# First batch's attention with keys on partitions, its maxima entered as a row and its probabilities kept in float32

## The chip, the core and the metric

The kernel runs on one core of a Trainium2 chip. The metric is the device time of one execution in microseconds (us). The engines of the core are named as the profile names them: PE (TensorE, matrix products; PEld is its weight loads), DVE (VectorE), ACT (ScalarE), POOL (GpSimd) and SP, whose queue issues the DMA transfers here. Each engine works through its own instructions in the order in which the built program lists them and waits on semaphores for the others.

## What is computed

```python
def _attn_ref(q, k, v, g_q, g_k):            # q, k, v: (4, 12, 448, 64)
    def rmsnorm(x, g):
        rms = np.sqrt(np.mean(x * x, axis=-1, keepdims=True) + 1e-06)
        return x / rms * g
    q_n, k_n = (rmsnorm(q, g_q), rmsnorm(k, g_k))
    scores = (1.0 / np.sqrt(64)) * np.matmul(q_n, k_n.transpose(0, 1, 3, 2))
    scores = scores - np.max(scores, axis=-1, keepdims=True)
    attn = np.exp(scores)
    attn = attn / (np.sum(attn, axis=-1, keepdims=True) + 1e-09)
    return np.matmul(attn, v).astype(np.float32)
...
x = attention, reshaped to (1792, 768)
g = x @ w_gate; x = (g * (1 / (1 + np.exp(-g))) * (x @ w_val)) @ w_out      # d_ff 1536
h = x @ w_in;   x = (h * np.cos(h)) @ w_out                                 # d_ff 2048
```

The weights arrive as 64-bit floats, and the kernel rebuilds 32-bit floats from their bits. Products are made to float32 accuracy from pairs of 16-bit parts ("hi" and "lo").

## The kernel before, in words

Batch 0's attention is computed first. Then, for each batch b, the first expansion layer of batch b (pieces of gate, val and out1 weights, `mm_piece`, lines 826 to 834) is recorded together with the attention of batch b+1. At the end come the second layer's `h` products and its output. A batch has six pairs of heads (g = 0 to 5 for batch 0, 6 to 11 for batch 1), a pair has seven tiles of 128 query rows (64 of each head of the pair), and n counts the tiles.

The recording loop calls `step(n, b)`, in which tables of offsets (`OFF`, chosen by `PH`) place the preparation of each pair, and `DEL` the steps behind the scores. After the recording a scheduler of the framework sets the final order on each engine by its own model of durations and by when buffers of the pools come free. So a changed table or pool moves instructions on all engines. `CF` holds a string of flags for each batch, which say what engine does an optional step.

For one pair of batch 0 the steps before are these:

- Preparation: `p_load`, `p_vload`, squares and row sums (`p_sq`), a power on POOL (`p_pow`, 305), scaling (`p_mul`, 342/343/345; times the gains, 352), splits in hi and lo (357 to 377), a DMA transpose of q and k (`p_T`), and `p_sw`, which copies the transposed q with its halves exchanged to W (388, 389). `p_vhi` and `p_vlo` split v (396, 405).
- Scores, queries on partitions: four products of 64 columns each (`s_mm`, 419), the maximum of each row over the keys on DVE (`s_max`, 428), which is turned into a bias (430), and the exponential with the bias and with a running sum (`s_exp`, 438).
- Probabilities: split in hi and lo (`s_phi`, 462 on ACT or 464 on DVE; `s_plo`, 471 on POOL or DVE), transposed by DMA so that keys lie on partitions (`s_pt`), and multiplied with the split v (`a_av`, 530).
- The reciprocals of the sums are spread over the partitions by a float32 product with ones (`a_sum` and `a_r`, 491, 503, 505), and `a_x` scales the result (540) and splits it (545 to 549) into the tile xy, X[g], which the first layer reads.

PSUM has eight banks: four of the pool ps_m (`mm`, the first layer), one of ps_t (`t`, the attention's output) and three of ps_s (`s`, scores and small products). All pools live for the whole program, so a piece of batch 0's first layer may run as soon as the three X tiles it reads are there.

Of the kernel before, what the change touches and what calls it, by code (L numbers as in the profile page):

```python
# [27 lines left out]
VM1 = 2  # L28
VMQ = 2
# [35 lines left out]
 {'load': -7,  # L65
  'vload': -6,
  'sqk': -5,
  'sqq': -5,
  'pow': -4,
  'mul': -3,  # L70
  'khi': -2,
  'klo': -2,
  'qhi': -2,
  'qlo': -2,
  'T': -1,
  'vhi': -1,
  'vlo': -1,
  'sw': -1},
# [42 lines left out]
PH = (1, 1, 1, 1, 0, 1, 3, 4, 5)  # L121
# [12 lines left out]
def kernel(ctx: ExitStack, tc, q, k, v, g_q, g_k, w_gate, w_val, w_out, w2_in, w2_out, out):  # L134
# [31 lines left out]
    ps_m = ctx.enter_context(tc.tile_pool(name="ps_m", bufs=4, space=PSUM))  # L166
# [31 lines left out]
    vsc = const.tile([P, 2 * B], F32, name="vsc")  # L198
    ynrm = const.tile([P, B * KX], F32, name="ynrm")
# [5 lines left out]
    junk = const.tile([P, S], BF16, name="junk")  # L205
# [61 lines left out]
    def p_load(g):  # L267
        rqk = pool("raw", g).tile([P, 2, NS, D], F32, tag="rqk", name="rqk")
        nc.sync.dma_start(rqk[:, 1], rows7(k, g))
        nc.sync.dma_start(rqk[:, 0], rows7(q, g))  # L270
        prep[g] = dict(rqk=rqk)

    def p_vload(g):
        rv = pool("rv", g).tile([P, 2, NS, D], F32, tag="rv", name="rv")
        b, p = divmod(g, NP)
        vs = v[b, 2 * p:2 * p + 2].rearrange("h (q t) d -> q h (t d)", t=NS)
        rv2 = rv.rearrange("p h t d -> p h (t d)")
        nc.sync.dma_start(rv2[:HP], vs)
        nc.sync.dma_start(rv2[HP:, :, :S - D], vs[:, :, D:])
        if "vw" in cfg(g):  # L280
# [27 lines left out]
    def v_max(b):  # L308
# [19 lines left out]
        nc.vector.tensor_copy(vsc[:, 2 * b:2 * b + 2], ps[:, :2])  # L328

# [54 lines left out]
    def p_sw(g):  # L384
# [3 lines left out]
        nc.vector.tensor_copy(W[:HP], T[HP:, :NS])  # L388
        nc.vector.tensor_copy(W[HP:], T[:HP, :NS])
# [160 lines left out]

    PREP = (
# [10 lines left out]
    LEAD = -min(OFF[ph(g)][nm] + NS * g for g in range(NP) for nm, f in PREP)  # L562

    def s_prep(n):
        for nm, f in PREP:
            for g in range(NPAIR):
                if NS * g + OFF[ph(g)][nm] == n:
                    f(g)
# [13 lines left out]
    def step(n, b):  # L582
        if NB * b <= n < NB * (b + 1):
# [298 lines left out]
    def fin_out1(b, c, ps):  # L882
        for f in range(2):
# [3 lines left out]
            nc.scalar.activation(junk[:, :S], t, AF.Square, accum_out=ynrm[:, b * KX + kt:b * KX + kt + 1])  # L887
# [112 lines left out]
    open_pool(start_ctx, **A0)  # L1000
    gtmp = start_ctx.enter_context(tc.tile_pool(name="gtmp", bufs=1)).tile([P, D], F32, name="gtmp")
    emit_consts(gtmp)
    step(-LEAD, 0)
# [11 lines left out]
    start_ctx.close()  # L1015
    g_ctx = ctx.enter_context(ExitStack())
# [154 lines left out]
```

## Time and profile before

| | |
|---|---|
| time of three runs, median (lowest to highest) | 1394.31 us (1391.92 to 1395.64) |
| the profiled execution | 1392.76 us |
| its span, first to last instruction | 1391.0 us |
| busy: PE, DVE, ACT, POOL | 1181.6, 879.5, 654.6, 440.6 us |

The profile is one execution on the chip. A row of a group names the line, the engine, the operation, what it writes and reads, the shapes, how many there are, the time that they kept the engine busy, and the mean of one. The granted clock of PE is given as a share of 2.4 GHz. Busy time over the whole span says little, because the program has stages with different limits: batch 0's attention alone, batch 0's first layer beside batch 1's attention, the same for the later batches, and the second layer.

### The profile page before, as it was taken

Reading aid. Unit: us, or ns where it says so; the run is one execution under the profiler, and the core shown is the slowest. Engines: PE = TensorE matmul, PEld = TensorE weight load, DVE = VectorE, ACT = ScalarE, POOL = GpSimd, SP = SyncE. Lnnn points to the kernel's source line nnn. Section 1 sums busy time; section 2 is a strip of 40 time slices with the busy share of each in tenths; the row PEclk is TensorE's granted clock in tenths of the full one; section 3 lists DMA queues with packets and bytes.
Section 4 is the critical chain, followed back from the end, with each engine's and each line's share of the span. In section 5 each row is a group of like instructions: output and inputs, shape, how many; then the busy total and the mean of one; then the engine's idle time right before and its main releaser. Section 6 shows DMA issues by size and latency. Waiting matters only on the chain. (4 is left out here: it accounts for less than half of the span.)

```text
span 1391.0 us, 18432 instructions
## 1 busy us (share of the span) xinstructions
PE 1181.6 (85%) x6448; PEld 671.3 (48%) x6448; DVE 879.5 (63%) x1633; ACT 654.6 (47%) x1324; POOL 440.6 (32%) x340
## 2 busy tenths in 40 slices
PE   1267587776789799998989999995999999999998
PEld 0122233333565344773436855772455555666665
DVE  7988879989995777547755178547777775200000
ACT  3677454656342456535554336446677776200000
POOL 4767635534851245314332011101323233000000
PEclk9877778788999899999999999997999999999999
DMA  9699677877899899999999998863100012633221
GB/s 260 174 202 209 158 222 206 215 202 200 238 341 354 169 237 222 246 355 223 207 231 226 305 324 285 292 215 102 35 12 12 24 57 63 221 120 101 63 87 40
DMA packets 297149, 259.28 MB, mean 186 GB/s; under 512 B 210016, under 2 KB 241760, under 8 KB 297056
## 3 DMA queue, kind: packets, MB, share of 16 engines
q1 hardware_dynamic: 297056, 258.11, 66.6%
q8 instruction: 50, 0.82, 0.3%
q14 instruction: 43, 0.35, 0.1%
HBM read 163.64 MB, written 44.87 MB: 150 GB/s over the span
## 5 line engine op out<-in xcount | busy, mean ns | idle before, releaser
L832 PE MATMUL mm<-xy,wp 128*128 128x448 f16 x960 | 347.7, 364 | 22.6 <-DVE tmp L868 7.5
L833 PE MATMUL mm<-xy,wp 128*128 128x448 f16 x960 | 348.1, 363 | 0.0
L834 PE MATMUL mm<-xy,wp 128*128 128x448 f16 x960 | 341.4, 362 | 4.4 <-DVE wp L702 4.4
L471 POOL TENSOR_TENSOR p<-pr,p 128x448 f16<-128x448 f32 x114 | 141.2, 1245 | 180.7 <-ACT p L462 94.8
L845 PEld LDWEIGHTS <-g 128*128 128x128 f16 x1344 | 131.5, 98 | 87.3
L438 ACT ACTIVATE pr<-s,sm,esc 128x448 f32<-128x448 f32 x168 | 120.0, 716 | 81.5 <-DVE sm L432 58.4
L832 PEld LDWEIGHTS <-wp 128*128 128x128 f16 x960 | 97.3, 102 | 117.8 <-issue 28.3
L833 PEld LDWEIGHTS <-wp 128*128 128x128 f16 x960 | 96.4, 100 | 102.6 <-issue 26.1
L834 PEld LDWEIGHTS <-wp 128*128 128x128 f16 x960 | 94.7, 100 | 101.8 <-issue 10.9
L977 POOL TENSOR_TENSOR g<-tmp,g 128x448 f16<-128x448 f32 x64 | 68.8, 1094 | 226.7 <-ACT g L976 144.6
L419 PE MATMUL s<-T 128*64 128x448 f16 x336 | 71.7, 416 | 52.3 <-ACT pr L438 37.6
L832 PE MATMUL mm<-g,wp 128*128 128x448 f32 x288 | 108.7, 377 | 6.4 <-ACT wp L772 5.4
L834 PE MATMUL mm<-g,wp 128*128 128x448 f32 x288 | 105.6, 375 | 7.7 <-POOL wp L773 7.7
L833 PE MATMUL mm<-g,wp 128*128 128x448 f32 x288 | 106.7, 370 | 0.0
L879 POOL TENSOR_TENSOR g<-tmp,g 128x448 fp32r<-128x448 f32 x48 | 60.8, 1275 | 144.4 <-ACT g L878 144.1
L428 DVE TENSOR_REDUCE sm<-s 128x1 f32<-128x448 f32 x168 | 100.3, 613 | 5.9 <-PE s L419 5.5
L845 PE MATMUL s<-wp,g 128*128 128x384 f16 x576 | 100.3, 326 | 0.0
L845 PE MATMUL mm<-wp,g 128*128 128x384 f16 x576 | 99.1, 326 | 0.0
L305 POOL TENSOR_TENSOR ri<-ss,half 128x14 f32<-128x14 f32 x24 | 65.2, 2719 | 74.0 <-DVE ss L303 51.3
L462 ACT ACTIVATE p<-pr 128x448 f16<-128x448 f32 x132 | 73.1, 569 | 22.5 <-DMA PT<-p 19.3
L669 DVE TENSOR_SCALAR w<-raw 128x768 int32<-128x768 int32 x68 | 45.1, 667 | 53.3 <-DMA raw<-in_moe_w_out_dram 49.6
L670 DVE SCALAR_TENSOR_TENSOR w<-raw,w 128x768 int32<-128x768 int32 x68 | 75.1, 1112 | 0.7
(136 smaller groups left out, 1868.9 us busy)
## 6 DMA issues: line engine op xcount, KB each, us to landing
wp<-scr_out SPq DMA_DIRECT2D x96, 384.0 KB, 4.5
raw<-in_moe_w_out_dram SPq DMA_DIRECT2D x28, 768.0 KB, 6.5
wp<-scr_gate SPq DMA_DIRECT2D x36, 384.0 KB, 5.2
wp<-scr_val SPq DMA_DIRECT2D x36, 384.0 KB, 5.3
raw<-in_moe_w_in_dram SPq DMA_DIRECT2D x16, 768.0 KB, 6.2
raw<-in_moe_w_gate_dram SPq DMA_DIRECT2D x12, 768.0 KB, 5.3
raw<-in_moe_w_val_dram SPq DMA_DIRECT2D x12, 768.0 KB, 5.5
scr_out<-wp SPq DMA_DIRECT2D x24, 384.0 KB, 5.9
```

Source lines behind the costliest of these rows:

```text
L305: nc.gpsimd.tensor_tensor(ri.rearrange("p a b -> p (a b)"), ss, half[:, :2 * NS], op=ALU.pow)
L419: nc.tensor.matmul(ps[hs, :S].rearrange("p (t q) -> p t q", q=HP), (T, W)[i][:, t, hs], T[:, NS:, hs], start=(i == 0), stop=(i == 1),)
L428: nc.vector.tensor_reduce(sm[:, 0, t:t + 1], slot[n][:, :S], axis=AX.X, op=ALU.max)
L438: nc.scalar.activation(e, slot.pop(n)[:, :S], AF.Exp, bias=sm[:, 1, t:t + 1], scale=esc, accum_out=sm[:, 2, t:t + 1],)
L462: nc.scalar.activation(hi, slot[n], AF.Copy)
L471: eng.tensor_sub(p16[:, t - t0, 1], slot.pop(n), p16[:, t - t0, 0])
L670: nc.vector.scalar_tensor_tensor(wi, hi, -0x40000000, wi, op0=ALU.bitwise_and, op1=ALU.bitwise_or)
L832: nc.tensor.matmul(ps[f][:, :S], wh[:, s], x[:, 0], start=(first and i == 0), stop=False)
L833: nc.tensor.matmul(ps[f][:, :S], wh[:, s], x[:, 1], start=False, stop=False)
L834: nc.tensor.matmul(ps[f][:, :S], wl[:, s], x[:, 0], start=False, stop=(last and i == n - 1))
L845: nc.tensor.matmul(ps[:, :CO], x[:, a, p0:p0 + P], rhs, start=st, stop=sp)
L977: nc.gpsimd.tensor_sub(x[:, 1], r, x[:, 0])
```

## The change

Batch 0's attention gets a path of its own (`c_step` and the functions `c_*`); batches 1 to 3 keep theirs.

- `c_s` makes a tile of scores with queries on partitions as before, with two products in place of four, for the maximum alone. `c_row` takes the seven maxima of a pair, splits them in two 16-bit parts, turns them into rows with seven small products against an identity, and ACT copies them under the transposed q (B, rows 64 to 127).
- `c_st` makes the scores again, now with keys on partitions: one product for the hi parts and one for the lo part of k and the maxima's rows in the same 128 rows of contraction. ACT takes the exponential and writes it in float32. No split, no DMA transpose of the probabilities and no running sum.
- `c_av` multiplies the float32 probabilities with v and with ones, both as float32 products. The sums so arrive already spread over the partitions, in a bank of their own (u). `c_x` adds 1e-9, takes the reciprocal of the whole 128x448 tile on DVE, and scales.
- For batch 0 the gains and the lo part of k go to POOL, v is not split, and k is loaded head by head.
- `CF` of batch 1 changes too: the copies of W go to ACT (`sa`), all tiles' hi parts of the probabilities to ACT, R's copy (505) and the hi part of x (545) to ACT, the last part of v to a DMA, and the lo part of x (549) to POOL; the lo parts of k and q and one lo tile of the probabilities come to DVE; and q's scaling (343) moves to POOL.
- The four ps_m banks are opened only after batch 0's attention; until then three banks ps_c and one ps_u take their place.
- `fin_out1` squares in place in PSUM, and the tile `junk` is gone.

```diff
-A0 = {'raw0': 2, 'rv0': 1, 'h160': 1, 'T0': 1, 'p160': 3, 'pr0': 4, 'sq0': 3}
+A0 = {'raw0': 2, 'rv0': 2, 'h160': 1, 'sq0': 1, 'pr0': 6, 'T0': 1}
+COL = {'B': 3, 'C': 3, 'w': 3, 'r': 1}
...
-CF = ('rp rv vw ql vh nm xl qm qd qe b c e 2', 'rp rv vw ql vh nm xh kl qd qe c d e', 'ql xl 0 2 5 6', 'ql xl 0 3 4 6')
+CF = ('kl xl ql qm kg', 'rp vh nm xl qm sa 2', 'ql xl 0 2 5 6', 'ql xl 0 3 4 6')
...
+CAV = 1
+CXX = 8
+CSM = 10
+CRW = 2
+CSH = 10
...
-PH = (1, 1, 1, 1, 0, 1, 3, 4, 5)
+PH = (2, 2, 2, 2, 2, 2, 3, 4, 5)
...
-    ps_m = ctx.enter_context(tc.tile_pool(name="ps_m", bufs=4, space=PSUM))
...
-        nc.vector.tensor_copy(W[:HP], T[HP:, :NS])
-        nc.vector.tensor_copy(W[HP:], T[:HP, :NS])
+        if "sa" in cfg(g):
+            nc.scalar.activation(W[:HP], T[HP:, :NS], AF.Copy)
+            nc.scalar.activation(W[HP:], T[:HP, :NS], AF.Copy)
+        else:
+            nc.vector.tensor_copy(W[:HP], T[HP:, :NS])
+            nc.vector.tensor_copy(W[HP:], T[:HP, :NS])
...
+    def c_copy(g):
...
+        nc.vector.tensor_copy(Bq[:HP], T[HP:, :NS])
+        nc.vector.tensor_copy(T[HP:, :NS], T[:HP, :NS])
+        nc.scalar.activation(C[:HP], T[:HP, NS:], AF.Copy)
+
+    def c_s(n):
...
+        for h in range(2):
+            hs = slice(HP * h, HP * h + HP)
+            nc.tensor.matmul(ps[hs, :S].rearrange("p (t q) -> p t q", q=HP), T[:, t, hs], T[:, NS:, h::2], start=True, stop=True)
+        nc.vector.tensor_reduce(pg["m"][:, 0, t:t + 1], ps[:, :S], axis=AX.X, op=ALU.max)
+
+    def c_row(g):
...
+        nc.vector.tensor_scalar(W[:, :, 0], m, 2.0 ** -14, None, op0=ALU.mult)
+        nc.vector.scalar_tensor_tensor(W[:, :, 32], m, 2.0 ** -14, W[:, :, 0], op0=ALU.mult, op1=ALU.subtract)
+        for t0, t1 in ((0, 4), (4, NS)):
+            ps = bank(ps_s, "s")
+            for t in range(t0, t1):
+                nc.tensor.matmul(ps[HP:, (t - t0) * P:(t - t0 + 1) * P], W[:, t], id16, start=True, stop=True)
+            nc.scalar.activation(
+                pg["B"][HP:, t0:t1], ps[HP:, :(t1 - t0) * P].rearrange("p (t q) -> p t q", q=P), AF.Copy,
+            )
+
+    def c_st(n):
...
+        for k, (wt, off, mv) in enumerate(((T, NS, T), (C, 0, Bq))):
...
+                nc.tensor.matmul(
+                    ps[rows, :S].rearrange("p (t q) -> p t q", q=HP), w, mv[:, :NS, hs], start=(k == 0), stop=(k == 1),
+                )
+        nc.scalar.activation(e, ps[:, :S], AF.Exp, scale=esc)
+
+    def c_av(g, j):
...
+        for dst, v_of in ((pg["o"], True), (pg["u"], False)):
+            for h in range(2):
...
+                nc.tensor.matmul(dst[hs, :S], w, e[rows], start=(j == 0), stop=(j == 3))
+
+    def c_x(g):
...
+        nc.vector.tensor_scalar(r, pg["u"][:, :S], 1e-9, None, op0=ALU.add)
+        nc.vector.reciprocal(r, r)
...
+        nc.vector.scalar_tensor_tensor(xs, pg["o"][:, :S], vs2, r, op0=ALU.mult, op1=ALU.mult)
+        nc.scalar.activation(x[:, 0], xs, AF.Copy)
+        nc.gpsimd.tensor_sub(x[:, 1], xs, x[:, 0])
...
-            nc.scalar.activation(junk[:, :S], t, AF.Square, accum_out=ynrm[:, b * KX + kt:b * KX + kt + 1])
+            nc.scalar.activation(ps[f][:, :S], ps[f][:, :S], AF.Square, accum_out=ynrm[:, b * KX + kt:b * KX + kt + 1])
...
     start_ctx.close()
+    ps_m = ctx.enter_context(tc.tile_pool(name="ps_m", bufs=4, space=PSUM))
```

What the built programs list shows the moves at three places. The first is PE in the middle of batch 0's attention, where probabilities meet v. Before (t is the output, PT the transposed probabilities, vh the hi part of v):

```order
L419 MATMUL s<-T,W 64x448
L419 LDWEIGHTS W
L419 MATMUL s<-T,W 64x448
L530 LDWEIGHTS vh
L530 MATMUL t<-PT,vh 64x448
```

After (pr are the float32 probabilities, rv is v, c the transposed scores):

```order
L641 LDWEIGHTS T
L641 MATMUL c<-T 128x448
L641 LDWEIGHTS cC
L641 MATMUL c<-cB,cC 128x448
L658 MATMUL t<-pr,rv 64x448
L658 MATMUL u<-pr,full 64x448
```

Where a run of 16-bit products stood (22 of line 530 for a pair), whose two halves of columns alternate, two float32 products for the same half of the columns (line 658, one to t and one to u) now follow each other, and 128-column score products stand between them and the next two.

The second place is DVE where a pair of batch 0 ends. Before (R spreads the reciprocals, p are the split probabilities):

```order
L487 TENSOR_SCALAR sm<-sm 128x7
L505 COPY R<-s 128x448
L488 RECIPROCAL sm<-sm 128x7
L428 TENSOR_REDUCE sm<-s 128x1 x2
L464 CAST p_754<-pr 128x448
L464 CAST p_787<-pr 128x448
L471 TENSOR_TENSOR p_787<-pr,p_787 128x448
L540 SCALAR_TENSOR_TENSOR tmp<-t,R 128x448
```

After (cr is the new tile of reciprocals, sm the maxima):

```order
L663 TENSOR_SCALAR cr<-u 128x448
L309 TENSOR_REDUCE ss<-sq 128x7
L612 TENSOR_REDUCE sm<-s 128x1
L664 RECIPROCAL cr<-cr 128x448
L612 TENSOR_REDUCE sm<-s 128x1
L598 COPY cB<-T 64x896
L309 TENSOR_REDUCE ss<-sq 128x7
L612 TENSOR_REDUCE sm<-s 128x1 x2
L667 SCALAR_TENSOR_TENSOR tmp<-t,vs_102,cr 128x448
```

The casts and the subtraction are gone, the reciprocal is over 448 elements in place of 7, and maxima of later tiles queue behind it.

The third place is PE where the first layer begins. Before, in the middle of batch 0's attention (mm are the first layer's banks, wp its weights):

```order
L503 MATMUL s<-R,ones 128x448
L832 LDWEIGHTS wp
L832 MATMUL mm<-xy,wp 128x448
L833 LDWEIGHTS wp
L833 MATMUL mm<-xy,wp 128x448
```

After, at the end of batch 0's attention:

```order
L658 MATMUL t<-pr,rv 64x448 x2
L658 MATMUL u<-pr,full 64x448 x2
L843 MATMUL s<-nm,full 128x1
L979 LDWEIGHTS wp
L979 MATMUL mm<-xy,wp 128x448
L980 LDWEIGHTS wp
L980 MATMUL mm<-xy,wp 128x448
```

All of the first layer's products now stand behind the last of batch 0's attention, where in the program before they were interleaved with its second half.

## Rows read from the trace of the kernel before

**Rows 1.** Stages: window, length, busy time of each engine (instructions), PEclk, DMA share, GB/s.

```profile
0.00:157.00 157.00, 70.71 (x372) 28.86 (x373) 133.43 (x242) 92.78 (x220) 102.36 (x86) 0.83 0.88 207
157.00:425.00 268.00, 198.83 (x970) 108.36 (x968) 242.34 (x375) 136.15 (x298) 141.69 (x92) 0.84 0.83 230
425.00:900.00 475.00, 441.80 (x2463) 261.72 (x2464) 301.38 (x656) 224.40 (x477) 127.77 (x98) 0.97 0.93 260
```

**Rows 2.** Timeline of DVE: batch 0's first and last scaling by the reciprocals.

```profile
84.37 0.62 DVE L540 SCALAR_TENSOR_TENSOR tmp<-t,R 128x448 f32<-128x448 f32 x1
...
156.74 0.62 DVE L540 SCALAR_TENSOR_TENSOR tmp<-t,R 128x448 f32<-128x448 f32 x1
```

**Rows 3.** Groups by line, DVE, 0 to 425 us: busy, mean ns | idle before.

```profile
L428 DVE TENSOR_REDUCE sm<-s 128x1 f32<-128x448 f32 x89 | 53.2, 612 | 3.3 <-PE s L419 2.9
...
L464 DVE CAST p<-pr 128x448 f16<-128x448 f32 x36 | 22.1, 616 | 3.5 <-ACT pr L438 3.2
...
L405 DVE SCALAR_TENSOR_TENSOR vl<-rv,vsc,vh 128x256 f16<-128x256 f32 x28 | 19.3, 722 | 2.8 <-ACT sq L295 1.6 <-ACT vh L396 1.2
L345 DVE TENSOR_TENSOR rqk<-rqk,ri 128x896 f32<-128x896 f32 x10 | 15.5, 1547 | 0.6 <-POOL ri L305 0.6
L352 DVE TENSOR_TENSOR rqk<-rqk,gk 128x448 f32<-128x448 f32 x16 | 14.9, 929 | 0.1
L389 DVE COPY W<-T 64x896 f16<-64x896 f16 x14 | 10.7, 762 | 0.2
L388 DVE COPY W<-T 64x896 f16<-64x896 f16 x14 | 9.6, 683 | 3.0 <-DMA T<-h 2.6
...
L505 DVE COPY R<-s 128x448 f32<-128x448 f32 x12 | 7.4, 615 | 3.6 <-PE s L503 3.5
...
L363 DVE TENSOR_TENSOR h<-rqk,h 128x448 f16<-128x448 f32 x9 | 7.1, 793 | 0.0
L471 DVE TENSOR_TENSOR p<-pr,p 128x448 f16<-128x448 f32 x8 | 6.9, 864 | 1.3 <-ACT p L462 1.2
L487 DVE TENSOR_SCALAR sm<-sm 128x7 f32<-128x7 f32 x12 | 5.8, 481 | 0.1
L342 DVE TENSOR_TENSOR rqk<-rqk,ri 128x448 f32<-128x448 f32 x6 | 5.5, 924 | 0.0
L281 DVE COPY rv<-rv 64x128 f32<-64x128 f32 x12 | 5.0, 416 | 2.0 <-DMA rv<-in_v_dram 1.7
L549 DVE TENSOR_TENSOR xy<-tmp,xy 128x448 f16<-128x448 f32 x6 | 4.4, 736 | 0.0
...
L545 DVE CAST xy<-tmp 128x448 f16<-128x448 f32 x6 | 2.9, 489 | 0.0
L488 DVE RECIPROCAL sm<-sm 128x7 f32<-128x7 f32 x12 | 2.3, 190 | 0.1
L681 DVE RECIPROCAL wsc<-winv 128x1 f32<-128x1 f32 x12 | 1.9, 157 | 0.2
```

**Rows 4.** Timeline of PE: a float32 product at either clock, and pairs behind one.

```profile
73.53 1.83 PE L503 MATMUL s<-R,ones 128*128 128x448 f32 x2 [0.22 <-ACT pr L438]
75.30 0.58 PE L419 MATMUL s<-T 128*64 128x448 f16 x2
75.67 0.42 PE L419 MATMUL s<-T,W 128*64 128x448 f16 x2
...
200.88 0.92 PE L503 MATMUL s<-R,ones 128*128 128x448 f32 x2
201.63 0.28 PE L696 MATMUL s<-nm,full 128*128 128x1 f32 x2
```

**Rows 5.** Groups by line, ACT, 0 to 425 us: a copy of 896 columns.

```profile
L396 ACT ACTIVATE vh<-rv,vsc 128x896 f16<-128x896 f32 x12 | 12.3, 1034 | 2.6 <-PE t L530 2.0 <-DVE rv L281 0.6
```

**Rows 6.** Timeline of DVE: one copy of W while POOL is idle.

```profile
37.81 0.39 DVE L388 COPY W<-T 64x896 f16<-64x896 f16 x1
```

**Rows 7.** DMA issues, 0 to 157 us: count and median us to landing.

```profile
PT<-p SPq DMA_TRANSPOSE x24, 4.3
```

More of the change, by code (lines that the diff above doesn't have):

```diff
@@ L64 @@
   'sw': -5},
[L65 to L78, printed above, removed]
+ {'load': -23,
+  'vload': 2,
+  'sqk': -18,
+  'sqq': -18,
+  'pow': -15,
+  'mul': -15,
+  'khi': -15,
+  'klo': -11,
+  'qhi': -14,
+  'qlo': -9,
+  'T': -3,
+  'vhi': -10,
+  'vlo': -4,
+  'sw': -2},
  {'load': -13,
@@ L198 @@
     vsc = const.tile([P, 2 * B], F32, name="vsc")
+    vs2 = const.tile([P, 1], F32, name="vs2")
+    id16 = const.tile([P, P], F16, name="id16")
     ynrm = const.tile([P, B * KX], F32, name="ynrm")
@@ L549, in a_x, with ctile, c_const @@
         eng.tensor_sub(x[:, 1], xs, x[:, 0])
+    col = {}
+    colc = {}
+    CT = [(0, 0), (1, 0), (0, 1), (1, 1), (0, 2), (1, 2), (None, 3)]
+    def ctile(nm, shape, dt, g=None):
+        return c_p.tile(shape, dt, tag="c" + nm, name="c" + nm, bufs=COL[nm])
+    def c_const(i):
+        C = ctile("C", [P, NS, P], F16)
+        nc.vector.memset(C[HP:], 0.0)
+        for r in (HP, HP + 32):
+            nc.vector.memset(C[r:r + 1], -(2.0 ** 14))
+        W = ctile("w", [P, NS, HP], F16)
+        nc.vector.memset(W, 0.0)
+        colc[i] = (C, W)
@@ new lines, in c_st @@
+    def c_st(n):
+        g, i = divmod(n, NS)
+        pg = prep[g]
+        T, Bq, C = pg["T"], pg["B"], colc[g % 3][0]
+        ps = bank(ps_c, "c")
+        h0, j = CT[i]
+        e = col[g, i] = pool("pr", g, n).tile([P, S], F32, tag="pr", name="pr")
+        for k, (wt, off, mv) in enumerate(((T, NS, T), (C, 0, Bq))):
+            for h in ((0, 1) if h0 is None else (h0,)):
+                hs = slice(HP * h, HP * h + HP)
+                rows = hs if h0 is None else slice(0, P)
+                k0 = (off + 2 * j) * P + h
+                w = wt.rearrange("p t q -> p (t q)")[:, k0:min(k0 + 2 * P - 1, (off + NS) * P):2]
+                nc.tensor.matmul(
+                    ps[rows, :S].rearrange("p (t q) -> p t q", q=HP), w, mv[:, :NS, hs], start=(k == 0), stop=(k == 1),
+                )
+        nc.scalar.activation(e, ps[:, :S], AF.Exp, scale=esc)
@@ new lines, in c_av @@
+    def c_av(g, j):
+        pg = prep[g]
+        if j == 0:
+            pg["o"] = bank(ps_t, "t")
+            pg["u"] = bank(ps_u, "u")
+        rv = pg["rv"]
+        for dst, v_of in ((pg["o"], True), (pg["u"], False)):
+            for h in range(2):
+                hs = slice(HP * h, HP * h + HP)
+                rows = slice(0, P) if j < 3 else hs
+                e = col[g, 2 * j + h] if j < 3 else col[g, NS - 1]
+                w = rv[rows, h, 2 * j if j < 3 else NS - 1 - h] if v_of else full[rows, :HP]
+                nc.tensor.matmul(dst[hs, :S], w, e[rows], start=(j == 0), stop=(j == 3))
@@ L560, in ph @@
         return PH[g if g < NP else NP - 1 + g // NP]
-    LEAD = -min(OFF[ph(g)][nm] + NS * g for g in range(NP) for nm, f in PREP)
+    LEAD = -min(OFF[ph(g)][nm] + NS * g - CSH for g in range(NP) for nm, f in PREP)
     def s_prep(n):
@@ L582, in step @@
     def step(n, b):
-        if NB * b <= n < NB * (b + 1):
+        if b == 0:
+            c_step(n)
+        elif NB * b <= n < NB * (b + 1):
             s_mm(n)
@@ L1000 @@
     open_pool(start_ctx, **A0)
+    ps_c = start_ctx.enter_context(tc.tile_pool(name="ps_c", bufs=3, space=PSUM))
+    ps_u = start_ctx.enter_context(tc.tile_pool(name="ps_u", bufs=1, space=PSUM))
+    c_p = start_ctx.enter_context(tc.tile_pool(name="cp", bufs=1))
     gtmp = start_ctx.enter_context(tc.tile_pool(name="gtmp", bufs=1)).tile([P, D], F32, name="gtmp")
     emit_consts(gtmp)
+    for i in range(3):
+        c_const(i)
     step(-LEAD, 0)
```

62 lines of the change are left out of this document (57 added, 5 removed).

## The prediction

> **What bounds the kernel now.** First the table of stages [rows 1]. Until 157 us batch 0's attention runs nearly alone, until 425 us batch 0's first layer runs beside batch 1's attention, and from then on PE is busy 442 of 475 us at a clock of 0.97. In the first two stages DVE is the fullest engine: 133 of 157 us (85%) and 242 of 268 us (90%); PE has 71 and 199 us, ACT 93 and 136, POOL 102 and 142. A later stage that is full of PE work starts when the earlier ones end, so what is saved before 425 us should come out at the end nearly one to one. Then the pace within the first stage: batch 0's first pair is scaled at 84.4 us and its sixth at 156.7 [rows 2], so a pair takes 14.5 us. Then the groups of DVE [rows 3]: their idle time in front is small nearly everywhere, so DVE sets the pace by the work in its list. The question is therefore how much DVE work the change takes out before 425 us, and whether PE, which gets slow float32 products, takes over as the bound.
>
> **DVE, batch 0.** Removed for six pairs, each count times its mean [rows 3]: 18 casts of probabilities x 0.616 = 11.1 us, 6 subtractions (471) x 0.864 = 5.2, 12 lo parts of v (405) x 0.722 = 8.7, 6 products with the gains (352) x 0.929 = 5.6 and 6 lo parts of k (363) x 0.793 = 4.8, which both go to POOL, 6 copies of R (505) x 0.615 = 3.7, 6 additions to the sums (487) x 0.481 = 2.9, 6 small reciprocals x 0.190 = 1.1, 6 copies of v's last part (281) x 0.416 = 2.5. Together 45.6 us. The seven maxima of a pair (428), the scaling and two copies of 64x896 stay in kind and number. Added: 6 additions of 1e-9 over 128x448, like line 505, 3.7 us; 12 operations on 128x7 at about 0.2, 2.4 us; and 6 reciprocals over 128x448, which no row shows. Their bounds: 0.615 us, if a reciprocal runs like the copy of that size, and, by the slope between the reciprocal of one element (0.157) and of seven (0.190), 0.0055 us for an element, 0.15 + 448 x 0.0055 = 2.6 us. I take 2.6, because it rests on the same operation: 15.7 us. The memsets of the new constants stand at the very start, where DVE waits for the first loads; I take nothing, and up to 3 us if they are not covered. Net: 45.6 - 21.8 = 23.8 us less.
>
> The Trainium skill (VectorE: DVE Perf Modes, First, the fixed hardware budget) speaks against this part: it says that a reciprocal runs an iterated divide with a repeat count of 8, and gives DVE's clock as 0.96 GHz. By that an estimate is 448 x 8 / 0.96 GHz = 3.7 us for one and 6.6 us more for the six; no row here shows that size.
>
> **DVE, batch 1.** Removed: 18 casts, 11.1 us; 6 times the two copies to W (0.683 + 0.762), 8.7, which ACT takes over; 6 copies of R, 3.7; v's last part, 2.5; x's hi part (545) 6 x 0.489 = 2.9 and lo part (549) 6 x 0.736 = 4.4; the smaller scaling (1.547 - 0.924) x 6 = 3.7. Together 37.0 us. Added: lo parts of k and q, 12 x 0.793 = 9.5, and 6 subtractions x 0.864 = 5.2. Net 22.3 us less. Both batches: **46 us** of DVE work less, all before 425 us. The ends, with the reciprocal at 0.6 us and with uncovered memsets (3 us) beside a sum that is 10% off: 58 and 38.
>
> **Where it is missing.** Counting both lists of DVE to batch 0's last scaling, with these means, the new one is only about 8 us shorter there, because the conversion of weights and batch 1's preparation have moved ahead of it; by the end of the first layer's conversions the whole difference is there. So 8 us belong to the first stage and some 38 to the second.
>
> **PE, stage one.** A float32 product of 448 columns takes [rows 4] 1.77 us at the half clock (73.53 to 75.30) and 0.75 us at the full one (200.88 to 201.63). A 16-bit pair in the two column halves takes 0.37 us at the half clock (75.30 to 75.67) and half of that, 0.19, at the full one. A pair of heads had 14 + 11 such pairs and one float32 product: 25 x 0.19 + 0.75 = 5.5 us at the full clock. It now has 7 pairs of products for the maxima, 14 for the transposed scores, seven small ones (about 0.1 us each) and 16 float32 products, in the order that follows each tile's exponential, t and u for the same half of the columns in a row, so I count them one after the other: 21 x 0.19 + 0.7 + 16 x 0.75 = 16.7 us at the full clock and 21 x 0.37 + 0.7 + 16 x 1.77 = 37 us at the half clock. If t and u for different halves did overlap, as the 16-bit pairs do, it would be 10.7 and 23. For six pairs 100 us at the full clock, 221 at the half. The room for it is about 120 us: from the first scores, which come later (I take 30 us, since POOL does two more steps of the first pairs' preparation), to some 150. At the full clock that is 83% of the room; at the half clock it is far too much. The row of the stage [rows 1] has a clock of 0.83, that is about a third of the time at 1.2 GHz, for a PE that was busy 71 of 157 us. With PE busy most of the time I expect more of the full clock, and that PE and DVE become about equally tight. So I give the first stage nothing: the last scaling at about 157 us as before, where DVE alone would give 157 - 8 = 149.
>
> **Other engines and queues.** PE's first layer for batch 0 can no longer begin inside the first stage, since its banks are opened behind it; what moves is 72 products x 0.19 = 14 us of PE work into a stage with 199 of 268 us busy. ACT loses the running sums, biases and splits of batch 0 and gains in batch 1: 18 hi parts (0.57), 12 copies of W at most 1.03 each (the nearest row, line 396 [rows 5], has all partitions), 6 copies of R and 6 of x; some 28 us on 136. POOL loses batch 0's subtractions and gains three smaller steps. SP loses batch 0's 24 transposes of probabilities [rows 7], which delayed nobody but their own pair. The squares in PSUM (887) hold a bank some half microsecond longer, beside PE work on the other banks: nothing.
>
> **Sum.** Second stage: PE would have 199 + 14 us in 268 - 38 = 230 us (93% at the old clock, less if the clock rises), ACT 164 of 230. With three engines that full in fixed orders not all of DVE's 38 us will come through; I take four fifths, 30 us, because DVE's 90% is still above PE's share at a better clock. The profiled execution took 1392.76 us: 1392.8 - 0 - 30 = **1363 us**. The median of the runs shown is 1.5 us above that execution, well within what I can claim; 0.3% (4 us) is about what a measurement of this kernel can tell from no change.
>
> **Rivals.**
>
> More comes through: PE keeps the full clock in stage one and the last scaling comes at about 149, and the second stage yields its whole 38 us: 46 us, 1347 us. DVE's own operations may get shorter too: a copy to W takes 0.39 us while POOL is idle [rows 6] against a mean of 0.683 [rows 3], and POOL loses work; some 6 us, 1341. For it: DVE's small idle times. Against it: PE's 83%.
>
> Less comes through: in the second stage the first layer's pieces wait for weights, ACT and PE in turn, the DMA share is 0.83 already and the same bytes have to come in less time. Then about 10 us remain: 1383 us.
>
> Slower: PE becomes the bound of stage one at the half clock. Each float32 product waits for its tile's exponential and is followed by a wait for the next, so that PE is never busy for long. With a share s of the work at the half clock it has 100 + 121 s us; started at 30 us and with 7 us behind it, the last scaling comes at 137 + 121 s. It is at 157 for s = 0.17, and the second stage's 30 us are used up at 187, s = 0.41. With s = 0.55 it is 204, 47 - 30 = 17 us slower: 1410 us. For it: a third of this stage ran at the half clock. Against it: PE had less than half the work.
>
> No change: what the first stages gain is lost again after 425 us, for instance to a DMA share of 0.93 [rows 1]: 1392 us. Against it: PE is 93% busy there.
>
> **How the numbers follow.** Forecast, 1352 to 1376: 0.47. More: 0.17. Less: 0.16. No change: 0.06. Slower: 0.14. The likeliest case gives 1363. Leaving out the slower case and a tail of the greater gain, the range is 1340 to 1393, in which the unknown reciprocal (up to 12 us less) lies too. Faster 0.47 + 0.17 + 0.16 = 0.80, the same 0.06, slower 0.14.
>
> **What would show it.** Right: the reciprocal of 128x448 at about 2.6 us; float32 products for t and u some 0.75 us apart at the full clock; a clock above 0.83 until the last scaling, which comes between 145 and 168 us; the first piece of batch 1's first layer some 30 us earlier; the stage after that unchanged in length. Wrong: the last scaling beyond 187 us with a clock near 0.7 (slower), DVE well under 85% in the second stage with waits for PE or DMA in its place (less), or a stage after 425 us that grows by what was gained.

## The result, and the profile after

The changed kernel takes 1374.97 us (median of four runs, 1374.25 to 1379.06) against 1394.17 us (median of four): a ratio of 0.987, 95% interval 0.9846 to 0.9893, so 19 us faster. The forecast was 1363 us (1352 to 1376 for its likeliest case), the range 1340 to 1393. The profiled execution took 1375.23 us, its span is 1373.1 us.

The stages of the changed kernel, in the windows of [rows 1] and with the same columns:

```profile
0.00:157.00 157.00, 98.47 (x422) 32.68 (x423) 112.74 (x203) 73.10 (x127) 68.71 (x55) 0.97 0.51 143
157.00:425.00 268.00, 227.68 (x1166) 125.04 (x1163) 233.24 (x346) 160.84 (x346) 135.17 (x90) 0.90 0.89 251
425.00:900.00 475.00, 434.55 (x2406) 262.35 (x2405) 308.80 (x665) 223.69 (x475) 129.95 (x97) 0.96 0.93 263
```

In the first window PE went from 71 to 98 us and DVE from 133 to 113; the clock rose from 0.83 to 0.97, and the share of the transfers fell from 0.88 to 0.51. Batch 0's scalings on DVE answer to [rows 2]:

```profile
81.97 0.68 DVE L667 SCALAR_TENSOR_TENSOR tmp<-t,vs,cr 128x448 f32<-128x448 f32 x1
...
168.96 0.68 DVE L667 SCALAR_TENSOR_TENSOR tmp<-t,vs,cr 128x448 f32<-128x448 f32 x1
```

The sixth one comes at 169.0 and not at 156.7: **the first stage became 12 us longer**, and a pair takes (169.0 - 82.0) / 5 = 17.4 us in the mean where it took 14.5. The pairs aren't even: the six scalings stand at 82.0, 97.6, 110.4, 138.1, 146.4 and 169.0 us, before at 84.4, 100.9, 118.6, 129.9, 142.2 and 156.7. So the new form is 2 to 8 us ahead for three pairs and falls behind from the fourth on. For the stages behind it, the end of a batch's first layer is a better mark (the start of its last copy by `fin_out1`, line 885 before and 1032 after):

| end of (us) | before | after | difference |
|---|---|---|---|
| batch 0's attention (sixth scaling) | 156.7 | 169.0 | +12.3 |
| batch 0's first layer | 428.2 | 406.9 | -21.3 |
| batch 1's first layer | 612.6 | 596.9 | -15.7 |
| batch 2's first layer | 795.8 | 774.9 | -20.9 |
| batch 3's first layer | 926.5 | 910.1 | -16.4 |
| the span | 1391.0 | 1373.1 | -17.9 |

So the second stage gained 34 us, of which the first took 12, and what was there at 407 us came out at the end but for 3 us. Cut at these marks, the first three stages were, before:

```profile
0.00:156.70 156.70, 70.41 (x370) 28.66 (x370) 133.12 (x241) 92.48 (x219) 102.36 (x86) 0.83 0.88 207
156.70:428.20 271.50, 202.32 (x988) 111.27 (x987) 244.38 (x377) 137.05 (x300) 141.69 (x92) 0.84 0.83 230
428.20:612.60 184.40, 166.75 (x937) 97.93 (x936) 116.76 (x251) 85.16 (x191) 62.13 (x45) 0.95 0.98 253
```

and are, after:

```profile
0.00:169.00 169.00, 110.06 (x476) 37.73 (x477) 124.11 (x218) 79.88 (x142) 71.15 (x57) 0.97 0.53 146
169.00:406.90 237.90, 198.12 (x1016) 110.70 (x1014) 216.18 (x325) 149.62 (x321) 129.51 (x84) 0.89 0.88 250
406.90:596.90 190.00, 163.00 (x906) 95.20 (x906) 128.37 (x256) 87.02 (x195) 66.66 (x47) 0.93 0.95 254
```

In the second stage DVE lost 28 us of work and is still busy 91% of it. In the first it is down to 73%. In the third it is busy 12 us longer than before, and that stage is 6 us longer: some of what left the first two stages came back there. Over the whole execution DVE's busy time fell by 25.6 us (879.5 to 853.9), and not by the 37 us of the first two stages.

**What the new operations cost.** Groups of DVE, 0 to 425 us, with the columns of [rows 3]:

```profile
L664 DVE RECIPROCAL cr<-cr 128x448 f32<-128x448 f32 x6 | 17.7, 2948 | 0.1
...
L583 DVE MEMSET cC<- 1x896 f16 x6 | 4.8, 805 | 1.4 <-issue 0.9 <-DVE gk L232 0.2 <-DVE ss L309 0.2
...
L663 DVE TENSOR_SCALAR cr<-u 128x448 f32<-128x448 f32 x6 | 3.7, 624 | 11.1 <-PE u L658 11.1
```

The reciprocal takes 2.95 us. The float32 products on PE, which answer to [rows 4]:

```profile
65.17 0.97 PE L658 MATMUL t<-pr,rv 128*64 128x448 f32 x2
65.97 0.91 PE L658 MATMUL u<-pr,full 128*64 128x448 f32 x2
66.82 0.36 PE L641 MATMUL c<-T 128*128 128x448 f16 x1
```

One float32 product is a row of two records; t and u of the same column half start 0.80 us apart.

**Why the first stage starts late.** PE's first scores came at 24.95 us in the kernel before. In the changed kernel they come at 45.00; below them stand the waits of SP's queue until 60 us (time in all, times, longest):

```profile
45.00 1.33 PE L611 MATMUL s<-T 128*64 128x448 f16 x6 [14.61 <-DVE T L599]
```

```profile
SPq L591 <- POOL h L378: 16.4, 1, 16.4
```

SP's first transpose waits 16.4 us for a lo part of k (378) on POOL, is issued at 40.05, and scores follow at 45.0. POOL until then:

```profile
15.52 5.16 POOL L318 TENSOR_TENSOR ri<-ss,half 128x14 f32<-128x14 f32 x2 [12.80 <-DVE ss L316]
...
21.69 2.59 POOL L318 TENSOR_TENSOR ri<-ss,half 128x14 f32<-128x14 f32 x1
...
28.19 7.16 POOL L367 TENSOR_TENSOR rqk<-rqk,gk 128x448 f32<-128x448 f32 x1
...
39.00 2.01 POOL L378 TENSOR_TENSOR h<-rqk,h 128x448 f16<-128x448 f32 x2
```

Its first power starts at 15.5 us (9.9 before), three pairs' steps are interleaved, and one product with the gains (367) takes 7.16 us where another one of the same shape took 1.12.

**Why a pair is slow once it runs.** The timelines of PE and of DVE around the third scaling:

```profile
105.90 0.39 PE L611 MATMUL s<-T 128*64 128x448 f16 x2
111.20 0.95 PE L623 MATMUL s<-id,cw 128*64 128x128 f16 x7 [4.92 <-DVE cw L619]
```

```profile
105.87 2.95 DVE L664 RECIPROCAL cr<-cr 128x448 f32<-128x448 f32 x1
108.74 0.12 DVE L618 TENSOR_SCALAR cw<-sm 128x7 f16<-128x7 f32 x1
108.89 0.39 DVE L599 COPY T<-T 64x896 f16<-64x896 f16 x1
109.31 0.62 DVE L309 TENSOR_REDUCE ss<-sq 128x7 f32<-128x448 f32 x1
109.85 0.61 DVE L612 TENSOR_REDUCE sm<-s 128x1 f32<-128x448 f32 x1
110.38 0.68 DVE L667 SCALAR_TENSOR_TENSOR tmp<-t,vs,cr 128x448 f32<-128x448 f32 x1
110.97 0.18 DVE L619 SCALAR_TENSOR_TENSOR cw<-sm,cw 128x7 f16<-128x7 f32 x1
```

PE stands for 4.92 us before the maxima's row of a pair, because on DVE the row's two small steps (618, 619) stand behind and between other work, the reciprocal first. DVE in turn waits for PE: 11.1 us in front of line 663 for the six pairs, for the sums u. The two engines take turns. How much that costs PE, from its first scores to its last product of batch 0's attention (163.4 us), is shown by the stretch and by the rows' group in it:

```profile
45.00:163.40 118.40, 103.70 (x445) 34.30 (x445) 87.78 (x153) 71.08 (x129) 42.70 (x30) 0.96 0.45 121
```

```profile
L623 PE MATMUL s<-id,cw 128*64 128x128 f16 x42 | 4.4, 252 | 10.1 <-DVE cw L619 9.4 <-ACT cB L624 0.7
```

PE stands idle for 14.7 of the 118.4 us, 9.4 of them for DVE in front of two of the six rows (4.46 and 4.92 us). PE is busy for the other 103.7 us.

### The profile page after: what moved, and what is told of

It is laid out like the page before. It is cut to its first block, busy times and chain, and to the rows that moved or that the text cites. A ratio compares the mean times of both kernels' runs of the same rounds, so it can differ in the third digit from the quotient of the medians.

```text
span 1373.1 us, 18378 instructions
## 1 busy us (share of the span) xinstructions
PE 1213.2 (88%) x6550; PEld 676.5 (49%) x6550; DVE 853.9 (62%) x1562; ACT 654.6 (48%) x1270; POOL 402.6 (29%) x305
## 5 line engine op out<-in xcount | busy, mean ns | idle before, releaser
L979 PEld LDWEIGHTS <-wp 128*128 128x128 f16 x960 | 97.5, 102 | 107.9 <-issue 22.3
L457 ACT ACTIVATE pr<-s,sm,esc 128x448 f32<-128x448 f32 x126 | 90.3, 718 | 81.4 <-DVE sm L451 71.3
L490 POOL TENSOR_TENSOR p<-pr,p 128x448 f16<-128x448 f32 x72 | 88.6, 1235 | 136.6 <-ACT p L481 107.6
L1026 POOL TENSOR_TENSOR g<-tmp,g 128x448 fp32r<-128x448 f32 x48 | 66.3, 1394 | 128.9 <-ACT g L1025 128.8
L447 DVE TENSOR_REDUCE sm<-s 128x1 f32<-128x448 f32 x126 | 75.5, 614 | 6.3 <-PE s L438 5.9
L481 ACT ACTIVATE p<-pr 128x448 f16<-128x448 f32 x126 | 70.0, 571 | 14.2 <-DMA PT<-p 13.3
L438 PE MATMUL s<-T 128*64 128x448 f16 x252 | 50.9, 390 | 27.9 <-ACT pr L457 24.2
L1135 ACT ACTIVATE tmp<-mm,osc 128x384 f32<-128x384 f32 x8 | 4.6, 580 | 148.6 <-PE mm L992 147.7
```

The source lines that it names most:

```text
L447: nc.vector.tensor_reduce(sm[:, 0, t:t + 1], slot[n][:, :S], axis=AX.X, op=ALU.max)
L457: nc.scalar.activation(e, slot.pop(n)[:, :S], AF.Exp, bias=sm[:, 1, t:t + 1], scale=esc, accum_out=sm[:, 2, t:t + 1],)
L481: nc.scalar.activation(hi, slot[n], AF.Copy)
L490: eng.tensor_sub(p16[:, t - t0, 1], slot.pop(n), p16[:, t - t0, 0])
L979: nc.tensor.matmul(ps[f][:, :S], wh[:, s], x[:, 0], start=(first and i == 0), stop=False)
L1026: nc.gpsimd.tensor_sub(x[:, 1], a, x[:, 0].bitcast(F32))
```

## The experiments

Two kinds of edit were run. In seven runs the source was edited and the scheduler laid out the program anew. In the other five, called "order kept", the edit was made to the built program, behind the scheduler: the list of every engine stayed that of the changed kernel, and single instructions were made shorter or put in twice. Ratios are to the kernel before, run beside each of them (its medians lay between 1392.9 and 1395.0 us); the changed kernel's own is 0.987. Stages are read from one profiled execution of each.

**The second batch's settings alone** (the kernel before, with the new `CF` string of batch 1 and the branch `sa`):

```diff
-'rp rv vw ql vh nm xh kl qd qe c d e'
+'rp vh nm xl qm sa 2'
```

> The kernel before, with the second batch's settings of the change alone (its softmax reciprocal's spread copied by ScalarE, the swapped copies of T on ScalarE, q scaled on GpSimd, high parts of probabilities and of x back on ScalarE, low parts of k on VectorE); the first batch as before. Theory (the second stage of 157 to 428 us is bound by VectorE, and some 22 us of its work leave it): the sixth scaling within 3 us of 156.7, the second stage shorter by 15 to 22 us, total 1372 to 1380 us. Rival (the second stage gains only by what the first batch's new form does earlier or leaves out): within 0.4% of before, 1388 to 1399 us.

Measured: 1378.78 us, ratio 0.9886 (0.9865 to 0.9907), as the theory had it; the sixth scaling came 4.5 us late and not within 3. Its first two stages:

```profile
0.00:161.20 161.20, 77.54 (x397) 33.15 (x398) 138.06 (x247) 99.49 (x232) 104.90 (x85) 0.89 0.87 202
161.20:409.40 248.20, 200.75 (x994) 110.86 (x992) 217.78 (x331) 151.99 (x325) 137.29 (x86) 0.86 0.87 245
```

**The first batch's new form alone** (the changed kernel, with batch 1's `CF` string of before):

```diff
-'rp vh nm xl qm sa 2'
+'rp rv vw ql vh nm xh kl qd qe c d e'
```

> The changed kernel with the second batch's settings of before: the first batch's new form alone. Theory (by the run with the second batch's settings alone, 15 us of the 19 come from these settings, and the first batch's form is worth about 4): 1386 to 1394 us. Rival (as the prediction's sum had it, half of VectorE's relief, and so half of the gain, comes from the first batch): 1375 to 1383 us.

Measured: 1396.01 us, ratio 1.0003 (0.9986 to 1.0019): above both ranges, by 2 us above the theory's. The new form alone is worth nothing in the total. Its first two stages, in a profiled execution of 1390.20 us, one of the shortest of its twelve:

```profile
0.00:162.90 162.90, 103.06 (x454) 34.23 (x455) 112.63 (x206) 72.89 (x130) 70.68 (x58) 0.98 0.48 136
162.90:430.40 267.50, 211.30 (x1014) 113.58 (x1013) 245.23 (x379) 136.00 (x295) 143.09 (x92) 0.83 0.86 237
```

The two rows tell why. The new form takes 20.5 us from DVE (133.1 to 112.6), all of it in the first stage, which became 6 us longer all the same; the second stage has its old 245 us of DVE and its old length. The settings of batch 1 take 26.6 us from DVE in the second stage (244.4 to 217.8), and that stage is 23 us shorter. So nearly all of the gain, 15 of 19 us, is there without the new form of batch 0's attention. For the other 4 us (1378.8 against 1375.0) the two intervals overlap.

**DVE in the second stage, doubled** (order kept; in front of each of the 42 row maxima of batch 1, line 447, the same maximum into a tile that nothing reads):

```diff
+            if i.name in TWICE:
+                ...
+                new.append(_copy.replace(i, ..., outs=[...dead...], sync_info=...on_wait...))
             new.append(i)
```

> The changed kernel with its order of instructions kept, and in front of each of the 42 row maxima of the second batch (0.61 us each on VectorE) the same maximum once more, into a tile that nothing reads: 25.8 us more of VectorE in the second stage, nothing else. Theory (VectorE, 93 percent busy there, sets the second stage): the second batch's last scaling at 408 to 415 us where it was at 388.4, total 1390 to 1401 us. Rival (the second stage and those behind it follow the transfers of weights, 89 to 95 percent busy): last scaling up to 10 us later, total 1375 to 1383 us.

Measured: 1391.11 us, ratio 0.9989 (0.9973 to 1.0004); batch 1's last scaling at 403.9 (388.4 in the changed kernel), 4 us short of the theory's range, the total within it. So 25.8 us more of DVE, as sums of durations, cost 16 us, 0.62 us for each. Neighbouring steps overlap at their ends, and others became shorter: DVE's busy time up to the end of batch 0's first layer rose by 18.0 us (340.3 to 358.3), and by that measure the price is 0.9. The second stage:

```profile
170.60:422.20 251.60, 205.20 (x1025) 113.54 (x1024) 233.17 (x363) 150.03 (x320) 130.10 (x84) 0.86 0.83 236
```

Its length is 1.08 times DVE's busy time; it was 1.11 before, 1.10 after, 1.14 and 1.09 in the two runs above. The second stage follows DVE.

**The same one batch later** (order kept, batch 2's maxima; the edit against the run above):

```diff
-...; g < 2 * NP and TWICE.add(i.ins.name)
+...; 2 * NP <= g < 3 * NP and TWICE.add(i.ins.name)
```

> The changed kernel with its order of instructions kept, and in front of each of the 42 row maxima of the third batch the same maximum once more (0.61 us each): 25.8 us more of VectorE between 390 and 580 us, where VectorE is busy two thirds of the time and the transfers 94 to 97 percent. Theory (transfers bound that stage, VectorE's relief would be worth nothing there): the third batch's last scaling 0 to 6 us later than 579.9, total 1375 to 1382 us. Rival (each us of VectorE costs 0.6 us there as it did in the second stage): 12 to 18 us later, total 1388 to 1395 us.

Measured: 1385.09 us, ratio 0.9932 (0.991 to 0.9955): 10 us for 25.8 us of DVE, between the two bets; the third batch's last scaling came at 591.1, 11.3 us late, just short of the rival's range. That stage is not set by the transfers alone; DVE still counts there for 0.4, or 0.6 by its busy time (145.4 us in that stage, against 128.4).

**PE's float32 products cut** (order kept, 64 of 448 columns in the products behind the first key tiles, line 658):

```diff
-nc.tensor.matmul(dst[hs, :S], w, e[rows], start=(j == 0), stop=(j == 3))
+i = nc.tensor.matmul(...); j and short(i, S, 64)
```

> The changed kernel, every engine's order of instructions kept as it is; of the 16 float32 products of each pair with v and ones, the 12 behind the first key tiles run over 64 of their 448 columns (the rest of what they would add is left out). 12 products at 0.40 us (halves overlapping) to 0.75 us are cut by six sevenths, so 4.1 to 7.7 us of TensorE a pair. Theory (TensorE paces the first stage, and the second, whose VectorE queue follows behind, passes the gain on): the sixth scaling at 140 to 150 us where it was at 169.0, total 1350 to 1362 us. Rival A (VectorE or the start paces the first stage): sixth scaling at 163 to 169 us, total 1370 to 1376. Rival B (the first stage's end does not decide the total, the second stage waits for something else): sixth scaling at 140 to 150 us, total 1368 to 1376 us.

Measured: sixth scaling at 160.9, total 1372.91 us, ratio 0.9868 (0.9845 to 0.9891). No bet held: the scaling lies between their ranges, and the total, within those of both rivals, can't be told from the changed kernel's. From the first scores to the sixth scaling, this kernel and then the changed one:

```profile
45.00:160.90 115.90, 83.87 (x459) 34.29 (x460) 92.89 (x160) 72.70 (x131) 43.58 (x31) 0.83 0.52 138
```

```profile
45.00:169.00 124.00, 108.89 (x472) 37.13 (x473) 93.29 (x160) 72.08 (x131) 43.81 (x31) 0.96 0.49 130
```

PE is busy 25 us less, and the stage is 8 us shorter. Its clock fell from 0.96 to 0.83, so what is left runs slower, and DVE's 93 us now are 80% of the stretch. Up to PE's last product of batch 0's attention, which came at 152.7 in place of 163.4, it is

```profile
45.00:152.70 107.70, 78.69 (x444) 32.06 (x444) 84.69 (x151) 68.58 (x122) 41.31 (x29) 0.84 0.50 131
```

Of the 25 us, 10.7 came out as time and 14.3 as more waiting: PE stands idle for 29.0 us here and for 14.7 in the changed kernel. PE is 88% busy there in the changed kernel, but it isn't the bound by itself.

**The reciprocal cut** (order kept, 7 columns of 448, line 664):

```diff
-nc.vector.reciprocal(r, r)
+short(nc.vector.reciprocal(r, r), S, NS)
...
```

> The changed kernel with its order of instructions kept; the six reciprocals of 128x448 (2.95 us each) run over 7 columns, and the sums in front of them are set to one, so that the division is left out (the scale carries a thousandth to keep the range). 16.5 us of VectorE less in the first stage. Theory (TensorE paces it): sixth scaling at 163 to 169 us, total 1368 to 1376 us. Rival (VectorE paces it): sixth scaling at 152 to 157 us, total 1358 to 1366 us.

Measured: sixth scaling at 162.6, total 1372.38 us, ratio 0.9865 (0.9841 to 0.9888): nearly as the theory had it, far from the rival. 16.5 us of DVE less are 6.3 us at the end of the first stage, 2.4 at the end of batch 0's first layer (404.5), and nothing in the total that can be told from the spread.

**The start** (order kept, for three pairs q's scaling and the gains over 8 of 64 elements on POOL, lines 358 and 367):

```diff
...
-eng.tensor_tensor(k3, k3, gk..., op=ALU.mult)
+i = eng.tensor_tensor(k3, k3, gk..., op=ALU.mult); g < 3 and short(i, D, 8)
```

> The changed kernel with its order of instructions kept; for the first three pairs GpSimd's scaling of q and its product of k with the gains run over 8 of every 64 elements (the rest stays unscaled). These six steps took 17.5 us of GpSimd up to 39.0 us, and the short ones 1 to 5 us in all. Theory (GpSimd's chain releases the first transpose, and the start decides the first stage): first scores at 31 to 36 us where they were at 45.0, sixth scaling at 156 to 162 us where it was at 169.0, total 1362 to 1368 us. Rival A (the start has slack): sixth scaling at 166 to 169 us, total 1372 to 1376 us. Rival B (the first stage's end does not decide the total): sixth scaling at 156 to 162 us, total 1370 to 1376 us.

Measured: first scores at 41.3, sixth scaling at 164.5, total 1374.26 us, ratio 0.9875 (0.9855 to 0.9894). No bet held. The six steps took 13.5 us in the changed kernel's trace and not 17.5, and 3.3 us here; the scores came only 3.7 us earlier, since another step of POOL now took the long time (below); but those 3.7 us are 4.4 at the sixth scaling and 4.2 at 402.7, where batch 0's first layer ends. The start has no slack as far as these 3.7 us show. In the total nothing of it can be told from the spread. Taken together, the three runs ended batch 0's first layer at 400.8, 404.5 and 402.7 us, 6.1, 2.4 and 4.2 before the changed kernel's 406.9, and the totals are too coarse to say what is left of that.

**The same three questions, laid out anew.** Gains and lo part of k of three pairs on DVE; the reciprocal left out; products with ones for the first key tiles alone:

```diff
-eng = nc.gpsimd if "kg" in cf else nc.vector
+eng = nc.gpsimd if "kg" in cf and g > 2 else nc.vector
...
-eng = nc.gpsimd if "kl" in cfg(g) else nc.vector
+eng = nc.gpsimd if "kl" in cfg(g) and g > 2 else nc.vector
```

> The changed kernel, with the gains and the low part of k of the first three pairs on VectorE and not on GpSimd (six GpSimd steps fewer before the sixth scaling, about 4.3 us more of VectorE: six steps of 0.68 to 0.76 us). Theory (the first stage starts late because GpSimd's chain of preparation releases the first transpose at 40 us, and from there on TensorE's pace of 17.4 us a pair sets the rest): first scores at 28 to 36 us where they were at 45.0, every scaling earlier by about as much, the sixth at 154 to 162 us where it was at 169.0, total 1360 to 1369 us. Rival (the first stage is paced by VectorE, and the start has slack): first scores earlier, the sixth scaling at 167 to 173 us, total 1373 to 1379 us.

```diff
-nc.vector.tensor_scalar(r, pg["u"][:, :S], 1e-9, None, op0=ALU.add)
-nc.vector.reciprocal(r, r)
+nc.vector.tensor_scalar(r, pg["u"][:, :S], 1e-6, None, op0=ALU.mult)
```

> The changed kernel without the reciprocal of the sums: the addition in front of it becomes a multiplication, and the six reciprocals of 128x448 (2.95 us each, 17.7 us of VectorE) are left out, so the products are not divided. Theory (TensorE sets the pace of the first stage after its start): the sixth scaling earlier by no more than the last pair's own reciprocal, 163 to 169 us; what VectorE is rid of shows in the second stage at most in part, total 1364 to 1376 us. Rival (VectorE sets the pace): the sixth scaling earlier by five or six reciprocals, 151 to 155 us, total 1355 to 1362 us.

```diff
-nc.tensor.matmul(dst[hs, :S], w, e[rows], start=(j == 0), stop=(j == 3))
+if v_of or j == 0:
+    nc.tensor.matmul(dst[hs, :S], w, e[rows], start=(j == 0), stop=(j == 3 or not v_of))
...
```

> The changed kernel with the products with ones for the first key tile of each half only: 6 of the 16 float32 products of each pair are left out (the sums then lack three of four parts, and 1 is added to them in place of 1e-9). Theory (TensorE's float32 products pace the first stage): 6 products at 0.40 us (halves overlapping) to 0.75 us (one after the other) are 2.4 to 4.5 us a pair, so five pairs shorten by 12 to 22 us, the sixth scaling at 147 to 157 us, total 1353 to 1365 us. Rival (VectorE or the start sets the stage): the sixth scaling at 165 to 170 us, total 1371 to 1379 us.

Measured: 1378.24 us (0.9894, 0.9871 to 0.9917), 1377.06 (0.9878, 0.9855 to 0.9902) and 1384.64 (0.9928, 0.9908 to 0.9948). The sixth scaling came earlier in all three, at 164.9, 158.8 and 161.1, between the ranges of theory and rival each time (the first run's scores came at 40.9, not at 28 to 36), and none is faster than the changed kernel; the third, which only leaves work out, is 10 us slower. The second against its near twin with the order kept shows how that comes; first laid out anew, then with the order kept:

```profile
0.00:158.80 158.80, 103.75 (x452) 35.62 (x453) 104.89 (x207) 77.07 (x136) 68.28 (x55) 0.95 0.52 147
158.80:419.60 260.80, 205.46 (x1040) 114.14 (x1039) 232.79 (x335) 154.38 (x331) 138.48 (x88) 0.89 0.88 249
```

```profile
0.00:162.60 162.60, 105.52 (x462) 35.40 (x463) 107.35 (x217) 80.07 (x142) 72.12 (x57) 0.96 0.52 147
162.60:404.50 241.90, 198.51 (x1030) 112.17 (x1028) 217.18 (x325) 150.09 (x321) 131.59 (x84) 0.91 0.87 249
```

The new layout has ten DVE instructions more in the second stage (x325 to x335) and 15.6 us more of DVE there, so batch 0's first layer ends 15 us later although its attention ended 4 us earlier. Its first stage has ten fewer, six of them reciprocals that are left out; in both stages together DVE is busy 13 us longer for as many instructions. At the end of the execution the two are 3.5 us apart (spans of 1374.9 and 1371.4), so most of what the order cost at this mark was made up later. These three runs say how far the scheduler's order can move the time, and nothing on what bounds the first stage.

**Two tries for a faster kernel.** Batch 1's lo part of k, and the lo part of one tile of its probabilities, to POOL:

```diff
-'rp vh nm xl qm sa 2'
+'rp vh nm xl qm sa kl'
```

> The changed kernel with the second batch's low part of k (0.68 us) and the low part of one tile of its probabilities (0.62 us) on GpSimd in place of VectorE: six of each, 7.8 us of VectorE less in the second stage, 12 to 14 us of GpSimd more, which is busy there for half of the time. Theory (0.62 us of total for each us of VectorE there, as the doubled maxima gave): 4.8 us less, 1368 to 1372 us. Rival (GpSimd, on which the transposes of the probabilities and TensorE wait, becomes late, or the new order of instructions costs as much): 1374 to 1382 us.

Measured: 1389.42 us, ratio 0.9973 (0.9954 to 0.9992), 14 us lost, more than theory or rival had. Its first two stages, in a profiled execution of 1394.99 us, one of the longest of its twelve:

```profile
0.00:165.90 165.90, 105.67 (x454) 35.47 (x455) 119.25 (x211) 78.64 (x139) 70.20 (x58) 0.97 0.51 146
165.90:419.60 253.70, 206.51 (x1038) 111.72 (x1037) 222.27 (x319) 151.71 (x325) 147.65 (x97) 0.89 0.87 241
```

DVE has 13 instructions fewer in both stages together than the changed kernel (530 against 543), and 341.5 us of busy time against 340.3: POOL's 18 us more in the second stage came with DVE's other steps running longer, by as much as was saved. Order and contention aren't separated here.

The copies to W on ACT for batches 2 and 3 too:

```diff
-'ql xl 0 2 5 6', 'ql xl 0 3 4 6'
+'ql xl sa 0 2 5 6', 'ql xl sa 0 3 4 6'
```

> The changed kernel with the swapped copies of T on ScalarE for the third and fourth batch too: 24 VectorE copies of 0.39 us at least, up to 1.9 us where GpSimd works beside them (9.4 us by the least, some 15 us as the changed kernel's mean has it), against 24 of 0.95 us on ScalarE, which is busy there for less than half of the time. Theory (0.4 us of total for each us of VectorE there, as the third batch's doubled maxima gave): 4 to 6 us less, 1369 to 1371 us. Rival (the new order of instructions that the scheduler makes of it costs as much or more, as it did when six steps went to GpSimd): 1373 to 1385 us.

Measured: 1375.81 us, ratio 0.9876 (0.9846 to 0.9906): no difference, as the rival had it. No version was found that beats the changed kernel.

## Why the prediction was right, and where it was not

- **DVE's work.** Batch 1: 22.3 us less in the sum; with its settings alone DVE lost 21.7 us over both stages. Batch 0: 23.8 in the sum; the form alone took 19.6. Both together took 37 of the 46. The reciprocal was 2.95 us and not 2.6, and the six one-partition memsets (4.8 us) were not covered: the first sums of squares stand among them. Each size held within some 4 us, their sum within 9. The estimate of 3.7 us that was worked out from the Trainium skill (VectorE: DVE Perf Modes, First, the fixed hardware budget) is 0.75 us above what the trace shows for a reciprocal, the slope between two rows 0.35 us below it.
- **Where the relief goes.** This is the step that failed. The sum put 8 us in the first stage and 38 in the second; measured are 9 and 28. But with the form alone DVE's relief stays in the first stage and turns into idle time there, and the total does not move. The second stage's gain comes with batch 1's settings.
- **"I give the first stage nothing": +12 us.** Two things were wrong in that term. The first scores were taken at 30 us and came at 45, as POOL's chain releases the first transpose at 40. And PE's 100 us for six pairs, near what it turned out to be (103.7 us busy from 45.0 to 163.4, with some work for batch 1 among it), do not run back to back: PE waits for rows behind DVE's reciprocal, DVE for PE's sums. With 45 for 30, the formula of the slow rival becomes 152 + 121 s, which gives 157 us at the stretch's clock of 0.96 (8% of the time and so 4% of the work at the half clock). The other 12 us are PE's idle time of 14.7 us, less smaller terms (5.6 us behind PE's last product where the formula has 7, and 1 us of PE's work). In the trace 9.4 of the 14.7 are waits for DVE in front of rows; the two runs that cut one side of the alternation ended the stage 8 and 6 us earlier. The slow rival's own cause, the half clock, did not come: 0.97 from the start to 169 us.
- **Four fifths of 38.** 30 us were forecast for the second stage and 34 measured, but on 28 us of relief. The fraction was too low and the relief too high. The run with batch 1's maxima doubled puts a price on it from the other side: 0.62 us of total for 1 us of DVE by durations, 0.9 by busy time.
- **The rest unchanged.** 17.9 of the 21.3 us at batch 0's first layer arrive at the end, as [rows 1] was read to say. But the stage behind it did change: it grew by 5.6 us, with 12 us more of DVE. With batch 1's settings alone it is much the same: 21.7 us of DVE less up to that mark, 10.1 us less over the whole execution (879.5 to 869.5).
- **The signs and the luck.** The clock held (0.97), t and u start 0.80 us apart, the reciprocal is 2.95 us. The last scaling at 169.0 is 1 us past the 145 to 168 of the forecast, and batch 0's first layer ends 21 us earlier where the forecast has the next one begin some 30 earlier. The way and the size came out because batch 1's settings were in the sum as well: four fifths of their 22.3 us are 18 us by themselves, near the 19 measured. That the total still lay within the range, though the new form gave nothing, is owed to the width of the range.
- **Left open:** how much of the 15 us of batch 1's settings is relief and how much a luckier order. The price of 0.62 on 22.3 us gives 14 us, and 0.9 on the 21.7 us of busy time gives 19, so relief is enough to explain it. But in two of the runs that were laid out anew (the reciprocal left out; more on POOL) batch 0's first layer ended 13 us later than in the changed kernel with no more for DVE to do, and no run of batch 1's settings keeps the order of the kernel before.

## What to carry to other kernels

Ask of each us that a change takes from an engine in which stage it is taken, and take it at its price only where that engine's busy time sets the stage's length; here 1 us of the same engine was worth 0.6 us or more in one stage, and in the stage ahead of it 16.5 us less gave 6 at its end and 2 behind it. Where a scheduler lays out the program, test a cause on the built program with its order kept: nearly the same edit, laid out anew, ended the next stage 15 us later and the whole 3.5 us later. And when steps move to another engine at the very start, follow the chain to the first product that needs them, and not the sum of work.

## What the runs showed of the hardware

- A POOL step took some six times its usual time while DVE worked without a gap. Line 367 took 7.16 us from 28.19, while DVE was busy 7.07 of the 7.10 us from 28.2 to 35.3, mostly with steps that read two tiles, such as these:

```profile
28.29 0.94 DVE L817 SCALAR_TENSOR_TENSOR w<-raw,w 128x768 int32<-128x768 int32 x1
...
31.42 0.61 DVE L357 TENSOR_TENSOR rqk<-rqk,ri 128x448 f32<-128x448 f32 x1
```

  When that step was made shorter, another one got the delay, in the run with the short start:

```profile
25.80 7.07 POOL L392 TENSOR_TENSOR h<-rqk,h 128x448 f16<-128x448 f32 x1
```

  The Trainium skill (SBUF — State Buffer, Who interferes with whom) says that a DVE instruction with two inputs in SBUF contends with a POOL instruction that reads SBUF, as the two engines share a pair of ports. The trace agrees as far as POOL's step lasted through fifteen DVE instructions in a row, some of them with one input; which of them held it no run here shows.
- With three quarters of the float32 products cut to 64 columns, PE's busy share fell from 88% to 72% and its granted clock from 0.96 to 0.83: 25 us less of PE work gave 8 us.
- A memset of one partition and 896 16-bit elements takes 0.805 us, more than a copy of 64 partitions of the same length (0.39 us).
